# Split factors for the first tile's h from chunk 6 on, splits made by GpSimd and accumulating transfers, in a linear attention with a rational feed-forward on one Trainium2 core

## The chip, the cores and the metric

The program runs on one core of a Trainium2 chip (trn2). The metric is the time of the whole program on the device in microseconds, as the median of several runs; profiles come from one execution each. The engines are PE (TensorE), ACT (ScalarE), DVE (VectorE), POOL (GpSimd) and SP (SyncE, which issues most transfers).

## The reference

```python
# q, k, v: 8 x 8 x 576 x 64 (batch, heads, seq, head_dim); w_in: 512 x 2048; w_out: 2048 x 512
kv = einsum('bhsd,bhse->bhde', k, v)
out = einsum('bhsd,bhde->bhse', q, kv)
out = out / sqrt(mean(out * out, axis=-1) + 1e-6) * g_norm
x = out.transpose(0, 2, 1, 3).reshape(4608, 512)
h = x @ w_in
P = a[0] + a[1] * h + a[2] * h**2 + a[3] * h**3
Q = 1.0 + abs(b[0]) * abs(h) + abs(b[1]) * h**2
return (P / (Q + 1e-6)) @ w_out
```

The inputs of the attention are float32; the weights reach the kernel as float64 words, two 32-bit words per number.

## The kernel before

The 4608 rows are worked in nine tiles of 512 (t), and d_ff in 16 chunks of 128 (c). A *slot* is one pair (t, c), in a fixed order; the loop near the end of the kernel writes one slot after the other, and every engine executes its instructions in the order in which they are written. In slot i the elementwise work of h(t, c) runs on ACT and DVE (`ew_a` to `ew_d`), PE adds the product of g of two slots before into four accumulators (`gemm2`, LAG = 2), takes a step of the attention of tile t + 1 (kvp, op, ms), and makes h of the next slot (`gemm1`). h lies in a PSUM tag of two buffers, so the h after next waits until DVE has read h for the last time (L495).

PE multiplies float32 in two ways. From *unsplit* factors a block of 128 x 128 x 512 is one float32 matmul (L471, L534; the trace shows two records of it). From *split* factors, where a number is the sum of a high and a low part in float32r, it is three matmuls (L475 to L477: high weight by low x, low by high, high by high). Before, all of tile 0 is unsplit, and all later tiles are split.

Weights come in 16 units of two chunks, `("wi", c)` of w_in and `("wo", c)` of w_out. A table, `schedule`, gives each unit the slots in which it is fetched by SP (1 MB of float64), converted to float32 and split; -1 stands for the start. Conversion before: ACT scales the high words (L192), GpSimd writes the signs (`signs`, L225), ACT scales the low words, DVE shifts (L229) and adds in two halves (L233). The manual dependence `beside` holds GpSimd's signs until DVE has made q (L487). A split before is ACT's copy to float32r (L246, the high part), GpSimd's negative of it (L253), and a transfer that adds the float32 value to this (L254, `accum_op=ALU.add`), which leaves the low part.

SBUF cells are named by tags: `g0` to `g7` take raw units and later high parts, `f0` to `f15` float32 units and later low parts, `xA` and `xB` the split x of a tile in two groups of two head pairs (`split`, L293), and x of tile 0, `x0`, lies in `xB`:

```python
xs[t, p // 2] = xpool.tile([P, 2, 2, TW], F32R, tag=("xA", "xB")[p // 2], name=f"x_{t}_{p}")
```

A tile's x can be written into its cell when the last h of the tile before has read that cell.

Of the kernel before, what the change touches and what calls it, by code (L numbers as in the profile page):

```python
# [24 lines left out]
def linear_attention_then_rational_ffn(  # L25
# [97 lines left out]


    schedule = {
        ("wi", 0): (None, None, 11),
        ("wi", 2): (None, None, 12),
        ("wo", 0): (None, None, 13),
        ("wi", 4): (-1, 0, 14),
        ("wo", 2): (-1, 1, 15),  # L130
        ("wi", 6): (-1, 2, 16),
        ("wo", 4): (-1, 3, 17),
        ("wi", 8): (0, 4, 18),
        ("wo", 6): (0, 5, 19),
        ("wi", 10): (1, 6, 20),
        ("wo", 8): (2, 7, 21),
        ("wi", 12): (3, 8, 22),
        ("wo", 10): (4, 9, 23),
        ("wi", 14): (5, 10, 24),
        ("wo", 12): (6, 11, 25),  # L140
        ("wo", 14): (7, 12, 26),
    }
# [7 lines left out]
    order = []
    for c in range(NF):
        order += [(("wo", c - c % 2), c % 2)]
        order += [(("wi", c + 3 - (c + 3) % 2), (c + 3) % 2)] if c + 3 < NF else []
    made = {k: order[2 * k:2 * k + 2] for k in range(NF - 3)}
    for k, part in zip(range(NF - 3, NF), order[2 * (NF - 3):]):
        made[k] = [part]

    def unsplit(t, c):  # L160
        return t == 0
# [1 line left out]

    raws, ups, w32, whl, gparts = {}, {}, {}, {}, {}

    def fetch_w(u):
        kind, c = u
        k = units.index(u) % NG  # L170
        raws[u] = wpool.tile([P, 2 * DM], I64, tag=f"g{k}", name=f"raw_{kind}{c}")
        src = w_in[c:c + 2].rearrange("c p k f -> p c (k f)") if kind == "wi" else \
            w_out[c:c + 2].rearrange("c p f -> p c f")
        to = raws[u].rearrange("p (c f) -> p c f", c=2)
        for js in ((slice(0, 1), slice(1, 2)) if u in units[:2] else (slice(0, 2),)):
            nc.sync.dma_start(to[:, js], src[:, js])
# [11 lines left out]
    def scale(engine, to, of, by):  # L188
        if engine == "V":
            DVE.tensor_scalar(to, of, by, None, ALU.mult)  # L190
        else:
            ACT.activation(to, of, AF.Copy, scale=by)  # L192

    def conv_a(u, part=both, engine="S"):
        low, high = words(u, part)
        scale(engine, f32(high), f32(high), 2.0**-112)
        to = low if u in units[:2] else ups[u].bitcast(U16).rearrange("p (f w) -> p f w", w=2)[:, part, 0]
        scale(engine, to, low.bitcast(U32), 2.0**-29)

    def room(u):  # L200
        kind, c = u
        if u not in ups:
            ups[u] = wpool.tile([P, 2 * DM], F32, tag=f"f{units.index(u)}", name=f"{kind}w{c}")
            for j in range(2):
# [10 lines left out]
    def conv_add(u, part):
        w = ups[u].bitcast(I32)[:, part]
        DVE.tensor_tensor(w, w, words(u, part)[0], ALU.add)

    def conv_b2(u, part):
        conv_or(u, part)  # L220
        conv_add(u, part)


    def signs(u):
        return POOL.tensor_scalar(room(u), f32(words(u, both)[1]), 0.0, None, ALU.mult)  # L225

    def conv_shift(u):
        high = words(u, both)[1]
        DVE.tensor_scalar(high, high, 3, None, ALU.logical_shift_left)  # L229

    def conv_c(u, part):
        w = ups[u].bitcast(I32)[:, part]
        DVE.tensor_tensor(w, w, words(u, part)[1], ALU.add)  # L233

    def gpart(k, j):
        if k not in gparts:
            gparts[k] = wpool.tile([P, 2, 2 * DM], F32R, tag=f"g{k}", name=f"parts{k}")
        return gparts[k][:, j]

    def split_w(u):  # L240
        kind, c = u
        i = units.index(u)
        w = ups.pop(u)
        fpart = lambda k, what: wpool.tile([P, 2 * DM], F32R, tag=f"f{k}", name=f"{kind}{what}{c}")
        wh = gpart((i + 2) // 2, i % 2) if i < NU - 2 else fpart(i + 2, "h")
        ACT.copy(wh, w)  # L246

        def rest():
            wl = gpart(0, i) if i < 2 else fpart(i - 2, "l")
            for j in range(2):  # L250
                js = slice(j * DM, (j + 1) * DM)
                whl[kind, c + j] = wh[:, js], wl[:, js]
            POOL.tensor_scalar(wl, f32(wh), -1.0, None, ALU.mult)  # L253
            POOL.dma_start(wl, w, accum_op=ALU.add)  # L254
        return rest

# [33 lines left out]

    def split(t, p):  # L293
# [4 lines left out]
        ACT.copy(xh, f)
        x.setdefault(t, []).append((xh, xl))

        def rest():
            DVE.tensor_tensor(xl, f, f32(xh), ALU.subtract)
        return rest
# [163 lines left out]
    def gemm1_part(t, c, ph, cs):  # L467
        for kc in range(NPAIR):
            ks = slice(kc * P, (kc + 1) * P)
            if t == 0:  # L470
                PE.matmul(ph, w32["wi", c][:, ks], x0[:, kc, cs], start=(kc == 0), stop=(kc == NPAIR - 1))  # L471
# [3 lines left out]
            PE.matmul(ph, wh, xl, start=(kc == 0), stop=False)  # L475
            PE.matmul(ph, wl, xh, start=False, stop=False)  # L476
            PE.matmul(ph, wh, xh, start=False, stop=(kc == NPAIR - 1))  # L477


    def ew_a(t, c, ph, w=TW):  # L480
        nm = f"{t}_{c}"
# [3 lines left out]
        ACT.activation(d, ph, AF.Square)  # L485
# [1 line left out]
        q_made = DVE.scalar_tensor_tensor(q, d, b1abs, q, ALU.mult, ALU.add)  # L487
# [171 lines left out]
    conv_b1(u1, one)  # L659
    conv_b2(u1, one)  # L660
    conv_b1(u1, two)
    conv_shift(u2)


    slots = [(t, c) for t in range(NTILE) for c in range(NF)]
    beside = mybir.DependencyInfo(mybir.DependencyClass.Sync, mybir.DependencyReason.DATA)
    ph = gemm1(0, 0)
    for i, (t, c) in enumerate(slots[:-1]):
        q_made = ew_a(t, c, ph)
        for u in at_slot(1, i + 1):  # L670

            tc.add_manual_dep(signs(u).ins, q_made.ins.name, beside, reason="signs beside h")
        if i:
            ew_d(*slots[i - 1])
# [84 lines left out]
```

## Time and profile before

| | |
|---|---|
| median of 3 runs | 895.58 us (895.52 to 895.6) |
| profiled execution | 895.59 us, of which the span from first to last instruction is 893.8 |
| PE, PEld busy | 886.1 us (99%), 680.1 us (76%) |
| DVE, ACT, POOL busy | 774.0 us (87%), 696.6 us (78%), 114.4 us (13%) |
| granted TensorE clock | 1.00 throughout |

PE is the row of matmuls, PEld that of weight loads, which overlap them. Busy times are means over stages with different limits: the change touches the first tile (some 20 to 140 us) and the slots around it, and what it is worth is read there. A row of the chain or of a timeline begins with its start and its duration in microseconds; `[1.10 <-DVE q L487]` is the idle time before it and what ended this. A row of waits gives the sum, the number of times and the longest. All line numbers are those of the kernel before.

### The profile page before, as it was taken

How to read it: one execution, taken by the hardware profiler on the slowest of the kernel's cores; microseconds unless marked ns; L12 is line 12 of the kernel's file. 1: busy time of each engine (PE TensorE's matmuls, PEld its weight loads, DVE VectorE, ACT ScalarE, POOL GpSimd, SP SyncE). 2: the span in 40 equal slices, each digit the busy share in tenths (PEclk: the TensorE clock that was granted, in tenths of full speed). 3: DMA queues.
4: the chain of work that ended last, by engine and by line, in shares of the span. 5: the costliest groups of instructions: out<-in, count | busy, mean ns of one | idle time of the engine just before them, and what ended most of it. 6: DMA issues, size and time to landing. Idle time of an engine off the chain costs nothing.

```text
span 893.8 us, 11734 instructions
## 1 busy us (share of the span) xinstructions
PE 886.1 (99%) x4294; PEld 680.1 (76%) x4294; DVE 774.0 (87%) x1223; ACT 696.6 (78%) x1171; POOL 114.4 (13%) x95
## 2 busy tenths in 40 slices
PE   8999999999999999999999999999999999999998
PEld 6444446878887888878887888788878887888886
DVE  3988898989978898889978997899779988898887
ACT  5898878988886788777877787768767887777665
POOL 2644465663000000000000000000000000000000
PEclk9999999999999999999999999999999999999999
DMA  9864047754230203220320132011201020201001
GB/s 366 351 259 177 25 95 187 177 101 102 70 123 19 49 20 110 83 49 1 130 79 23 30 118 84 12 49 71 72 13 49 0 71 12 49 1 47 1 1 48
DMA packets 26266, 74.30 MB, mean 83 GB/s; under 512 B 2592, under 2 KB 2592, under 8 KB 26208
## 3 DMA queue, kind: packets, MB, share of 16 engines
q1 hardware_dynamic: 23328, 64.10, 20.9%
q0 software_dynamic: 2304, 8.39, 5.0%
q10 hardware_dynamic: 576, 1.05, 0.3%
q8 instruction: 34, 0.56, 0.2%
q14 instruction: 24, 0.20, 0.1%
HBM read 55.58 MB, written 9.57 MB: 73 GB/s over the span
## 4 chain that ended last, share of the span: by engine, by line
PE 97%; DMA 1%; DVE 1%; ACT 0%; issue 0%; SPq 0%; DVEq 0%; ACTq 0%
PE h L475 14%; PE h L477 13%; PE h L476 13%; PE acc L538 13%; PE acc L539 13%; PE acc L540 13%; PE acc L534 6%; PE h L471 5%; PE kvp L332 2%; DMA first<-in_first_dram 1%; PE ms L400 1%; PE op L383 1%; PE op L384 1%; PE op L382 1%; PE op L378 0%; DVE x L658 0%
## 5 line engine op out<-in xcount | busy, mean ns | idle before, releaser
L475 PE MATMUL h<-x,parts 128*128 128x512 f32 (+1 forms) x516 | 203.5, 394 | 0.0
L477 PE MATMUL h<-x,parts 128*128 128x512 f32 (+1 forms) x516 | 200.3, 388 | 0.0
L485 ACT ACTIVATE d<-h 128x512 f32<-128x512 f32 x143 | 85.6, 599 | 146.1 <-PE h L477 144.3
L539 PE MATMUL acc<-wol,gh 128*128 128x512 f32 x508 | 197.7, 389 | 0.0
L487 DVE SCALAR_TENSOR_TENSOR q<-d,b1abs,q 128x512 f32<-128x512 f32 x143 | 107.2, 749 | 91.1 <-ACT q L486 90.2
L476 PE MATMUL h<-x,wil 128*128 128x512 f32 (+1 forms) x388 | 150.4, 388 | 0.0
L538 PE MATMUL acc<-parts,gl 128*128 128x512 f32 x384 | 149.4, 389 | 0.0
L540 PE MATMUL acc<-parts,gh 128*128 128x512 f32 x384 | 149.4, 389 | 0.0
L475 PEld LDWEIGHTS h<-x,parts 128*128 128x128 f32 x516 | 96.9, 188 | 25.5 <-DVE gl L522 5.9
L498 ACT ACTIVATE d<-q,bias 128x512 f32<-128x512 f32 x143 | 105.6, 739 | 12.8 <-DVE q L487 10.8
L488 ACT ACTIVATE u<-h,na 128x512 f32<-128x512 f32 x143 | 112.6, 787 | 0.0
L477 PEld LDWEIGHTS h<-x,parts 128*128 128x128 f32 x516 | 96.9, 188 | 20.5
L539 PEld LDWEIGHTS acc<-wol,gh 128*128 128x128 f32 x508 | 95.4, 188 | 19.8
L499 ACT ACTIVATE d<-d,bias 128x512 f32<-128x512 f32 x143 | 103.6, 724 | 4.7
L505 DVE SCALAR_TENSOR_TENSOR u<-u,na,d 128x512 f32<-128x512 f32 x143 | 106.7, 746 | 0.0
L495 DVE SCALAR_TENSOR_TENSOR u<-u,na,h 128x512 f32<-128x512 f32 x143 | 106.1, 742 | 0.6
L503 DVE SCALAR_TENSOR_TENSOR q<-q,d 128x512 f32<-128x512 f32 x143 | 98.5, 689 | 0.2 <-ACT d L499 0.2
L489 DVE TENSOR_TENSOR u<-u,h 128x512 f32<-128x512 f32 x143 | 98.0, 686 | 0.4
L486 ACT ACTIVATE q<-h,abg 128x512 f32<-128x512 f32 x143 | 98.0, 685 | 0.0
L511 DVE SCALAR_TENSOR_TENSOR u<-q,u 128x512 f32<-128x512 f32 x127 | 91.7, 722 | 2.4
L522 DVE TENSOR_TENSOR gl<-u,gh 128x512 fp32r<-128x512 f32 x127 | 86.9, 684 | 0.0
L521 ACT CAST gh<-u 128x512 fp32r<-128x512 f32 x127 | 80.3, 632 | 4.1 <-DVE u L511 4.1
(146 smaller groups left out, 1226.6 us busy)
## 6 DMA issues: line engine op xcount, KB each, us to landing
kvm<-in_kv_dram SPq DMA_DIRECT2D x28, 640.0 KB
raw_wo<-in_w_out_dram SPq DMA_DIRECT2D x8, 1024.0 KB
qr<-in_qT_dram SPq DMA_DIRECT2D x32, 256.0 KB
out_dram<-ob SPq DMA_DIRECT2D x16, 512.0 KB
rb<-rd SPq DMA_DIRECT2D x28, 256.0 KB
raw_wi<-in_w_in_dram SPq DMA_DIRECT2D x6, 1024.0 KB
wol<-wow POOLq DMA_DIRECT2D x8, 512.0 KB, 5.3
wil<-wiw POOLq DMA_DIRECT2D x6, 512.0 KB, 4.6
```

Source lines behind the costliest of these rows:

```text
L475: PE.matmul(ph, wh, xl, start=(kc == 0), stop=False)
L476: PE.matmul(ph, wl, xh, start=False, stop=False)
L477: PE.matmul(ph, wh, xh, start=False, stop=(kc == NPAIR - 1))
L487: q_made = DVE.scalar_tensor_tensor(q, d, b1abs, q, ALU.mult, ALU.add)
L488: ACT.activation(u, ph, AF.Identity, bias=na[:, 2:3], scale=na[:, 3:4])
L495: DVE.scalar_tensor_tensor(u, u, na[:, 1:2], ph, ALU.add, ALU.mult)
L498: ACT.activation(d, q, AF.Ln, bias=bias[:, 2:3], scale=QSC)
L499: ACT.activation(d, d, AF.Exp, bias=bias[:, 3:4], scale=-1.0)
L505: DVE.scalar_tensor_tensor(u, u, na[:, 0:1], d, ALU.add, ALU.mult)
L538: PE.matmul(o, gl[:, ss], wh, start=(c == 0), stop=False)
L539: PE.matmul(o, gh[:, ss], wl, start=False, stop=False)
L540: PE.matmul(o, gh[:, ss], wh, start=False, stop=(c == NF - 1))
```

## The change

- Tile 0's h is made from split w_in and split x from chunk 6 on (`EARLY = 6`): three float32r matmuls per block instead of one float32 matmul. Products with w_out stay unsplit in tile 0.
- Its x is split at the start into two groups, one in `xA`, one in a new cell `e`.
- A split is made by GpSimd and a transfer alone (`low_by_transfer`): two GpSimd passes and an accumulating transfer. ACT's copy goes. w_in 6 to 14 are split in slots 3 to 8, the other units from slot 9 on.
- GpSimd's signs go, and with them the manual dependence. ACT scales the high words by a rectifier (Prelu) with a slope that makes the negative side carry the sign; both scalings are in place. DVE shifts straight into the float32 unit and adds, for w_in 4 to 14 in one instruction over both chunks.
- Fetches, conversions and cells have a new order, and tile 1's x uses the two cells the other way round.

```diff
     schedule = {
...
+        ("wi", 4): (-1, 0, 12, "g3", "f3", ("f1", "f2")),
+        ("wi", 6): (-1, 1, 3, "g4", "f4", "g4"),
+        ("wo", 2): (-1, 1, 13, "g5", "f5", "g0"),
+        ("wi", 8): (-1, 2, 4, "g6", "f6", "g6"),
...
     def conv_a(u, part=both, engine="S"):
         low, high = words(u, part)
-        scale(engine, f32(high), f32(high), 2.0**-112)
-        to = low if u in units[:2] else ups[u].bitcast(U16).rearrange("p (f w) -> p f w", w=2)[:, part, 0]
-        scale(engine, to, low.bitcast(U32), 2.0**-29)
+        if u == units[0]:
+            scale(engine, f32(high), f32(high), 2.0**-112)
+        else:
+            ACT.activation(f32(high), f32(high), AF.Prelu, scale=2.0**-112, alpha=-(2.0**32))
+        scale(engine, low, low.bitcast(U32), 2.0**-29)
...
-        ACT.copy(wh, w)
...
+    def low_by_transfer(high, low, of):
+        POOL.tensor_scalar(high, of, 1.0, None, ALU.mult)
+        POOL.tensor_scalar(low, f32(high), -1.0, None, ALU.mult)
+        POOL.dma_start(low, of, accum_op=ALU.add)
...
-            xs[t, p // 2] = xpool.tile([P, 2, 2, TW], F32R, tag=("xA", "xB")[p // 2], name=f"x_{t}_{p}")
+            xs[t, p // 2] = xpool.tile([P, 2, 2, TW], F32R, tag=("xA", "xB")[p // 2 ^ (t == 1)], name=f"x_{t}_{p}")
...
-            if t == 0:
+            if t == 0 and c < EARLY:
                 PE.matmul(ph, w32["wi", c][:, ks], x0[:, kc, cs], start=(kc == 0), stop=(kc == NPAIR - 1))
...
+    for g, tag in enumerate(("xA", "e")):
...
+        low_by_transfer(xs[0, g][:, :, 0], xs[0, g][:, :, 1], x0[:, 2 * g:2 * g + 2])
...
-        for u in at_slot(1, i + 1):
-
-            tc.add_manual_dep(signs(u).ins, q_made.ins.name, beside, reason="signs beside h")
...
-        rest[2] += [lambda u=u: conv_shift(u) for u in shifts]
+        rest[2] += [lambda u=u: conv_b1(u, both) for u in shifts]
```

In the table the three numbers are the slots of fetch, conversion and split; then come the cells of the raw unit, the float32 unit and the parts. How the rows move, at three places:

On ACT in slot 1 (behind the copies of kv, ahead of h of chunk 2; raw_wo and raw_wi are raw units, wow the float32 unit), before:

```order
L192 ACTIVATE raw_wo_251<-raw_wo_251 128x1024
L192 ACTIVATE wow_338<-raw_wo_251 128x1024
L485 ACTIVATE d_2_408<-h_2_376 128x512
L486 ACTIVATE q_2_409<-h_2_376,abg 128x512
L488 ACTIVATE u_2_410<-h_2_376,na 128x512
```

and after:

```order
L195 ACTIVATE raw_wi_251<-raw_wi_251 128x1024
L188 ACTIVATE raw_wi_251<-raw_wi_251 128x1024
L195 ACTIVATE raw_wo_253<-raw_wo_253 128x1024
L188 ACTIVATE raw_wo_253<-raw_wo_253 128x1024
L466 ACTIVATE d_2_412<-h_2_375 128x512
L467 ACTIVATE q_2_413<-h_2_375,abg 128x512
L469 ACTIVATE u_2_414<-h_2_375,na 128x512
```

Slot 1 converts two units instead of one ahead of h of chunk 2, and slot 3 likewise.

On POOL, from the end of the start-up on (wow and wiw are float32 units, x_157 is x0, wihl the parts of a unit), before:

```order
L225 TENSOR_SCALAR wow_297<-raw_wo_155 128x1024
L225 TENSOR_SCALAR wiw_303<-raw_wi_245 128x1024
L225 TENSOR_SCALAR wow_338<-raw_wo_251 128x1024
L225 TENSOR_SCALAR wiw_370<-raw_wi_253 128x1024
L273 TENSOR_TENSOR kvl_135<-kvf,kvh_129 64x64 x2
```

and after:

```order
L234 TENSOR_SCALAR x_0_320<-x_157 128x2x512
L235 TENSOR_SCALAR x_0_320<-x_0_320 128x2x512
L236 DMA x_0_320<-x_157 128x2x512
L234 TENSOR_SCALAR x_1_324<-x_157 128x2x512
L235 TENSOR_SCALAR x_1_324<-x_1_324 128x2x512
L236 DMA x_1_324<-x_157 128x2x512
L254 TENSOR_TENSOR kvl_135<-kvf,kvh_129 64x64 x2
L234 TENSOR_SCALAR wihl_477<-wiw_408 128x1024
L235 TENSOR_SCALAR wihl_477<-wihl_477 128x1024
L236 DMA wihl_477<-wiw_408 128x1024
```

Where four signs stood, x is split in two groups, and w_in 6 behind it; the signs are gone.

On ACT at the change from tile 1 to tile 2 (xf is x in float32, x_2_0 and x_2_2 the two groups of tile 2's split x, h_1_15 the last h of tile 1), before:

```order
L499 ACTIVATE d_1_14_1813<-d_1_14_1813,bias_95 128x512 [waits Activation_49]
L298 CAST x_2_0_1853<-xf_2_0_1119 128x512 [waits PE_49]
L298 CAST x_2_0_1853<-xf_2_1_1235 128x512
L298 CAST x_2_2_1856<-xf_2_2_1380 128x512 [waits PE_49]
L298 CAST x_2_2_1856<-xf_2_3_1492 128x512
L485 ACTIVATE d_1_15_1866<-h_1_15_1840 128x512
```

and after:

```order
L479 ACTIVATE d_1_14_1877<-d_1_14_1877,bias_95 128x512 [waits Activation_49]
L279 CAST x_2_0_1917<-xf_2_0_1214 128x512 [waits PE_49]
L279 CAST x_2_0_1917<-xf_2_1_1325 128x512
L279 CAST x_2_2_1920<-xf_2_2_1466 128x512
L279 CAST x_2_2_1920<-xf_2_3_1573 128x512
L466 ACTIVATE d_1_15_1930<-h_1_15_1904 128x512
```

The second group waits for nothing of its own any more: the cell of the first group is now the one that the last h of tile 1 reads last.

More of the change, by code (lines that the diff above doesn't have):

```diff
@@ L12 @@
 U32 = mybir.dt.uint32
-U16 = mybir.dt.uint16
 AF = mybir.ActivationFunctionType
@@ L125, in linear_attention_then_rational_ffn @@
     schedule = {
[L126 to L141, printed above, removed]
[16 rows of a table added]
     }
     units = list(schedule)
-    NU = len(units)
-    NG = NU // 2
     def at_slot(step, k):
         return [u for u in units if schedule[u][step] == k]
[L152 to L158, printed above, removed]
+    made = {0: [("wo", 0, 0), ("wi", 2, 1)]}
+    for c in range(1, NF):
+        made[c] = [("wo", c - c % 2, c % 2)]
+    for c in range(4, NF, 2):
+        made[schedule["wi", c][1] + 1].append(("wi", c, None))
+    EARLY = 6
     def unsplit(t, c):
         return t == 0
-    raws, ups, w32, whl, gparts = {}, {}, {}, {}, {}
+    raws, ups, w32, whl = {}, {}, {}, {}
     def fetch_w(u):
         kind, c = u
-        k = units.index(u) % NG
-        raws[u] = wpool.tile([P, 2 * DM], I64, tag=f"g{k}", name=f"raw_{kind}{c}")
+        raws[u] = wpool.tile([P, 2 * DM], I64, tag=schedule[u][3], name=f"raw_{kind}{c}")
         src = w_in[c:c + 2].rearrange("c p k f -> p c (k f)") if kind == "wi" else \
@@ L202, in room @@
         if u not in ups:
-            ups[u] = wpool.tile([P, 2 * DM], F32, tag=f"f{units.index(u)}", name=f"{kind}w{c}")
+            ups[u] = wpool.tile([P, 2 * DM], F32, tag=schedule[u][4], name=f"{kind}w{c}")
             for j in range(2):
@@ L217, in conv_add @@
         DVE.tensor_tensor(w, w, words(u, part)[0], ALU.add)
[L219 to L238, printed above, removed]
     def split_w(u):
         kind, c = u
-        i = units.index(u)
         w = ups.pop(u)
[L244 to L255, printed above, removed]
+        cells = schedule[u][5]
+        if isinstance(cells, str):
+            hl = wpool.tile([P, 2, 2 * DM], F32R, tag=cells, name=f"{kind}hl{c}")
+            wh, wl = hl[:, 0], hl[:, 1]
+        else:
+            wh, wl = (wpool.tile([P, 2 * DM], F32R, tag=g, name=f"{kind}{n}{c}") for g, n in zip(cells, "hl"))
+        for j in range(2):
+            js = slice(j * DM, (j + 1) * DM)
+            whl[kind, c + j] = wh[:, js], wl[:, js]
+        low_by_transfer(wh, wl, w)
+    def low_by_transfer(high, low, of):
+        POOL.tensor_scalar(high, of, 1.0, None, ALU.mult)
+        POOL.tensor_scalar(low, f32(high), -1.0, None, ALU.mult)
+        POOL.dma_start(low, of, accum_op=ALU.add)
     kvslot = {}
@@ L486, in ew_a @@
         ACT.activation(q, ph, AF.Abs, scale=b0)
-        q_made = DVE.scalar_tensor_tensor(q, d, b1abs, q, ALU.mult, ALU.add)
+        DVE.scalar_tensor_tensor(q, d, b1abs, q, ALU.mult, ALU.add)
         ACT.activation(u, ph, AF.Identity, bias=na[:, 2:3], scale=na[:, 3:4])
@@ L490, in ew_a @@
         pend[t, c] = (d, q, u)
-        return q_made
     def ew_b(t, c, ph, fill):
@@ L636, in linear_attention_then_rational_ffn @@
     conv_b1(u0, one)
-    conv_b2(u0, one)
+    conv_or(u0, one)
+    conv_add(u0, one)
     conv_a(u0, two, "V")
@@ L646, in linear_attention_then_rational_ffn @@
     conv_add(u0, two)
-    signs(u2)
     conv_a(u1, one)
     conv_a(u1, two)
-    for u in at_slot(1, 0):
-        signs(u)
     conv_a(u2)
@@ L658, in linear_attention_then_rational_ffn @@
         DVE.scalar_tensor_tensor(x0[:, p], x0[:, p], ghalf, rb, ALU.mult, ALU.mult)
[L659 to L662, printed above, removed]
+    conv_b1(u1, both)
+    conv_add(u1, one)
+    conv_b1(u2, both)
+    for g, tag in enumerate(("xA", "e")):
+        xs[0, g] = xpool.tile([P, 2, 2, TW], F32R, tag=tag, name=f"x_0_{g}") if g == 0 else \
+            wpool.tile([P, 2, 2, TW], F32R, tag=tag, name=f"x_0_{g}")
+        low_by_transfer(xs[0, g][:, :, 0], xs[0, g][:, :, 1], x0[:, 2 * g:2 * g + 2])
+        x.setdefault(0, []).extend((xs[0, g][:, p, 0], xs[0, g][:, p, 1]) for p in range(2))
     slots = [(t, c) for t in range(NTILE) for c in range(NF)]
-    beside = mybir.DependencyInfo(mybir.DependencyClass.Sync, mybir.DependencyReason.DATA)
     ph = gemm1(0, 0)
     for i, (t, c) in enumerate(slots[:-1]):
-        q_made = ew_a(t, c, ph)
-        for u in at_slot(1, i + 1):
-            tc.add_manual_dep(signs(u).ins, q_made.ins.name, beside, reason="signs beside h")
+        ew_a(t, c, ph)
         if i:
@@ L676, in linear_attention_then_rational_ffn @@
         shifts = []
-        convs = [lambda u=u, j=j: (conv_b2 if u == u1 else conv_c)(u, (one, two)[j]) for u, j in made.get(i, [])]
+        convs = [lambda u=(k, n), j=j: conv_add(u, both if j is None else (one, two)[j]) for k, n, j in made.get(i, [])]
         ew_b(t, c, ph, convs[:1])
@@ L683, in linear_attention_then_rational_ffn @@
                 evacuate(slots[i - LAG][0])
-        for u in at_slot(2, i) if i >= NF else []:
-            rest[2].append(split_w(u))
+        for u in at_slot(2, i):
+            split_w(u)
         if i < 4:
@@ L698, in linear_attention_then_rational_ffn @@
         rest[2] += convs[1:]
-        for u in at_slot(2, i) if i < NF else []:
-            rest[2].append(split_w(u))
         if t == 0 and c == NF - 3:
```

12 rows, old and new, of the table schedule are left out of this document.

## The prediction

> **What bounds the kernel now.** I read the page first, then the chain that ended last, then the waits and the timelines of the places that the change touches.
>
> ```profile
> span 893.8 us, 11734 instructions
> PE 886.1 (99%) x4294; PEld 680.1 (76%) x4294; DVE 774.0 (87%) x1223; ACT 696.6 (78%) x1171; POOL 114.4 (13%) x95
> PE 97%; DMA 1%; DVE 1%; ACT 0%; issue 0%; SPq 0%; DVEq 0%; ACTq 0%
> ```
>
> PE is busy for 99% of the span and 97% of the chain: work taken from PE shortens the time by its full length wherever the others keep up, and a wait of PE lengthens it by its full length. In the chain, ordered by time, these pieces carry the sum:
>
> ```profile
> 29.29 0.76 DVE u L495
> 30.09 3.70 PE h L471 x8
> 61.64 0.73 PE kvp L332 x20
> 62.37 3.63 PE h L471 x8
> 128.44 3.43 PE h L471 x8
> 135.31 0.23 PE h L475
> ...
> 137.84 0.23 PE h L477
> 138.07 3.43 PE acc L534 x8
> ```
>
> An h chunk from unsplit factors (L471) takes 3.43 us; one from split factors (twelve pieces, L475 to L477) takes 138.07 - 135.31 = 2.76. PE has one wait behind the start-up, for DVE in front of h of chunk 2:
>
> ```profile
> PEld h L471 <- DVE u L495: 1.3, 1, 1.3
> ```
>
> **A. Split h, chunks 6 to 15.** Ten chunks go from 3.43 to 2.76 us: 10 x 0.67 = -6.7 us, all on PE.
>
> **B. Start.** Chunk 2 takes the PSUM buffer that DVE L495 releases.
>
> ```profile
> 24.33 1.17 DVE L209 TENSOR_SCALAR wiw<-raw_wi 128x512 int32<-128x512 int32 x1
> ...
> 26.36 0.69 DVE L217 CUSTOM_DVE_ANT_0 wiw<-raw_wi,wiw 128x1024 uint16<-128x1024 uint16 x1
> ...
> 27.31 0.70 DVE L229 TENSOR_SCALAR raw_wo<-raw_wo 128x1024 int32<-128x1024 int32 x1
> 24.16 1.15 ACT L192 ACTIVATE raw_wo<-raw_wo 128x1024 f32<-128x1024 f32 x1 [2.47 <-POOL wow L225]
> 26.41 0.58 ACT L485 ACTIVATE d<-h 128x512 f32<-128x512 f32 x1
> ```
>
> Five DVE instructions, from 24.33 to about 27.9 (27.31 and the step of 0.6 between rows), become three: a shift of 1024 (0.70), an addition (0.69), a shift (0.70). ACT no longer waits 2.47 us for GpSimd's signs. DVE's q could then start near 26.7, when ACT has made its inputs from h of chunk 0, instead of 27.9: 1.2 us earlier, which is nearly all of PE's 1.3. Bounds 0 and -1.3; since GpSimd now runs beside it (D), I take -1.1.
>
> **C. Chunk 6: is its split there in time?** Its second pass (low part of w_in) comes at 62.37 + 0.23, less 1.1: 61.5. Ahead of it: slot 1 now has two conversions on ACT, then DVE's addition at the end of slot 2, two GpSimd passes, and the transfer.
>
> ```profile
> 35.26 0.72 ACT L498 ACTIVATE d<-q,bias 128x512 f32<-128x512 f32 x1 [1.10 <-DVE q L487]
> 37.31 1.17 ACT L192 ACTIVATE raw_wo<-raw_wo 128x1024 f32<-128x1024 f32 x1
> ...
> 39.76 0.60 ACT L485 ACTIVATE d<-h 128x512 f32<-128x512 f32 x1
> 45.01 0.69 DVE L511 SCALAR_TENSOR_TENSOR g<-q,u 128x512 f32<-128x512 f32 x1
> 45.62 0.68 DVE L233 CUSTOM_DVE_ANT_0 wiw<-raw_wi,wiw 128x1024 uint16<-128x1024 uint16 x1
> 138.57 3.32 POOL L253 TENSOR_SCALAR wol<-parts 128x1024 fp32r<-128x1024 f32 x1 [2.84 <-ACT parts L246]
> 143.93 2.98 POOL L253 TENSOR_SCALAR wil<-parts 128x1024 fp32r<-128x1024 f32 x1 [0.84 <-ACT parts L246]
> 147.20 0.90 POOL L254 DMA_DIRECT2D wil<-wiw  x1 [0.30 <-POOL wil L253]
> wol<-wow POOLq DMA_DIRECT2D x1, 512.0 KB, 8.8
> wil<-wiw POOLq DMA_DIRECT2D x1, 512.0 KB, 4.5
> 55.24 0.38 SPq L176 DMA_DIRECT2D raw_wo<-in_w_out_dram  x1
> ```
>
> The two rows of transfers are DMA answers for 140 to 152 us, with loads and stores beside it, and for 185 to 187, alone. A conversion costs ACT 39.76 - 37.31 = 2.45 us. Slot 2 there starts at 39.76, less 1.2 (earlier start), plus 2.45, less 0.7 (most of the 1.10 wait is swallowed): about 40.3. So g of slot 2 ends near 45.70 + 0.55, or 0.7 later if one GpSimd pass stops DVE (D); I take 46.5. The addition, now of 2048 halfwords instead of 1024, takes twice the step of 0.6 between the two DVE rows: 47.7. GpSimd takes 2 x (3.15, the middle of its two rows, + 0.30 before the next): issue at 54.6. Landing 4.5 later is 59.1, no wait; 8.8 later is 63.4, a wait of 1.9. I take the late one, because a 1 MB weight load starts at the same moment (55.24) and the 8.8 had such company: +1.9. Bounds 0 and +5: the addition half a slot later, or the transfer wholly behind those loads. A first share of this wait can show one step earlier, at kvp of pair 2 (61.64 less 1.1), whose PSUM bank ACT has to empty: ACT comes there 2 x 2.45 - 1.2 - 0.7 = 3 us later than before.
>
> **D. What GpSimd's passes do to DVE.**
>
> ```profile
> 139.30 1.41 DVE L511 SCALAR_TENSOR_TENSOR g<-q,u 128x512 f32<-128x512 f32 x1
> 146.19 0.68 DVE L511 SCALAR_TENSOR_TENSOR u<-q,u 128x512 f32<-128x512 f32 x1
> 145.77 3.43 PE acc L534 x8
> 120.00:130.00 10.00, 10.00 (x25) 4.38 (x24) 9.82 (x16) 6.01 (x10) 6.72 (x4) 1.00 0.51 116
> ```
>
> The first row lies 0.7 us behind the start of C's pass at 138.57, the second meets none: a DVE instruction with two SBUF inputs that meets the beginning of a pass takes 1.41 instead of 0.68, 0.7 us more. The signs of before start beside instructions that read PSUM and meet none. Now slots 0 to 8 hold 14 passes (four for x, ten for w_in), up to 14 x 0.7 = 10 us of DVE; up to chunk 6 they are in C's 0.7, behind it attention leaves PE's slots longer than DVE's. In the last slots DVE is full (9.82 of 10; the row is PE, PEld, DVE, ACT, POOL, clock): per slot of 6.87 us 6.75, now 7.45 against 6.2 for PE. Over three slots it falls back 3.7 us; g of chunk 15, which ends at 139.30 + 1.41, is used by the chain's L534 at 145.77, 5.1 later. So 0 here, +3 at worst. [...]
>
> **E. New map of cells.** For tile 1 the two x tiles change cells, so tile 2's first x needs the cell that h of (1,15) reads last instead of first.
>
> ```profile
> 227.60 1.15 ACT L298 CAST x<-xf 128x512 fp32r<-128x512 f32 x2
> 228.96 1.15 ACT L298 CAST x<-xf 128x512 fp32r<-128x512 f32 x2 [0.21 <-PE h L477]
> 228.54 0.68 DVE L302 TENSOR_TENSOR x<-xf,x 128x512 fp32r<-128x512 f32 x1
> 233.47 0.68 DVE L522 TENSOR_TENSOR gl<-u,gh 128x512 fp32r<-128x512 f32 x1
> 234.21 0.50 PE L538 MATMUL acc<-woh,gl 128*128 128x512 f32 x1
> ```
>
> The first cast moves from 227.60 to 228.96 and ends at 229.6; DVE's subtraction goes from 228.54 to 229.6, and L522, behind it without a gap, from 234.15 to 235.2. PE takes its result at 234.21, so nothing is in hand: +1.05. Bounds 0 (a gap on DVE that I do not see) and +1.4.
>
> **Moved fetches, and the rest.** SP's queue keeps its length: w_in 6 goes ahead of w_out 2, w_out 4 behind w_in 10, and the last w_out between the stores of rd and the loads of rb; two x transfers of 512 KB join the loads at about 30 and 37 us. I cost this at 0, covered by the one to three slots of 7 us between a fetch and its conversion; with that cover gone, ACT would wait at its conversion, ahead of C's chain, and the wait would be C's. Two passes per unit instead of ACT's copy and one pass: ACT is freed of one copy per unit, in slots that PE bounds: 0. From slot 16 on a unit comes every second slot with two passes instead of every slot with one: the same number of stops. The sign by a rectifier instead of a copy: the same 1024 elements, 0 (bounds under the rivals).
>
> **Sum.** -6.7 - 1.1 + 1.9 + 0 + 1.05 = -4.85 us, against the profiled execution's 895.59, 0.01 above the median of the runs: 890.7.
>
> **Rivals.** Faster or slower means by over 0.2% (1.8 us), about what a measurement of this kernel can tell from none.
> - *All hidden* (C is 0): 888.8. For it: 4.5 us alone; against it: the loads beside it. 0.15.
> - *The gain is eaten at chunk 6* (C from 4.9 to 8): 893.8 to 896.9. For it: four steps in a row, each of which can only be late; against it: no transfer row above 8.8. 0.17.
> - *DVE late at the end of the tile* (D +3): 893.5. For it: 9.82 of 10; against it: 5.1 in hand. 0.05, mostly faster.
> - *Slower: the rectifier costs ACT more.* Two functions above differ by 0.14 us on 512 columns (26.41, 35.26), 0.3 for 1024; the far end is a change of tables.
>
> ```profile
> 2.88 1.28 ACT L67 ACT_TABLE_LOAD   x1 [2.88 <-issue]
> 32.35 0.56 ACT L485 ACTIVATE d<-h 128x512 f32<-128x512 f32 x1
> 59.95 0.58 ACT L485 ACTIVATE d<-h 128x512 f32<-128x512 f32 x1
> ```
>
> From h of chunk 1 to h of chunk 5 ACT took 27.6 us (32.35 to 59.95) with four conversions; with six it needs 27.6 + 2 x 2.45 = 32.5, and PE's four slots take 32.3 (30.09 to 62.37). Each 0.1 us per rectifier delays ACT by 0.6 with little in hand. At 0.3 that is 1.8 us and goes into C's wait; from about 1.1 on (6.6 us, and each later slot overfull too) it is slower, and with two table loads per use (2.56, 15 us in these slots) 900 to 910. Against it: the changed program lists one table load in all, as before. 0.11.
> - *Not what it says:* a missed dependence that keeps h as long as before; the program's rows show three passes per block. 0.03, no change.
> [...]
>
> **How the numbers follow.** The forecast has 0.47. Faster: 0.47 + 0.15 + 0.03 = 0.65; same: 0.17 + 0.02 + 0.03 = 0.22; slower: 0.11 + 0.02 = 0.13. The range goes from the hidden case with B at its bound and E smaller, 888.0, to most of the eaten case, 896.0.
>
> **What would show it.** h of chunk 6 to 15 at 2.75 us; no wait of PE for L495 at 29 us; a wait of 1 to 3 us near 61, for the transfer of low w_in, part of it perhaps for ACT before kvp; one of 1 us near 227 for DVE; rectifier rows of 1.15 to 1.2 us; DVE instructions of 1.4 us beside GpSimd in the first tile. Wrong it would be if the rectifier's rows are above 1.6, if transfers in 50 to 65 us take over 12 us, or if PE waits for g near 130.

## The result and the profile after

The changed kernel takes 905.95 us (median of 4 runs, 905.55 to 906.35) against 895.55 for the kernel before (895.5 to 895.6): a ratio of 1.0116 (95% interval 1.0099 to 1.0134), 10.4 us slower. Forecast were 890.7. These lines of the page after answer to the first three of the prediction: span, busy time by engine, and the chain's shares.

```profile
span 903.9 us, 11786 instructions
PE 882.2 (98%) x4334; PEld 686.3 (76%) x4334; DVE 792.7 (88%) x1214; ACT 677.3 (75%) x1155; POOL 133.5 (15%) x103
PE 81%; DVE 13%; ACT 3%; issue 2%; DMA 1%; SPq 0%; DVEq 0%; ACTq 0%
```

PE's busy time is less by 3.9 us, where A had 6.7 (the run without weight passes below has 879.7, so 6.4 less; the matmuls of tile 0 take 2.5 us more here than there). DVE, with nine instructions fewer than before, is busy 18.7 us longer, and now carries 13% of the chain (1% before). The windows say where. Columns: stretch, length, then busy time (and instructions) of PE, PEld, DVE, ACT, POOL, then clock and DMA. First before, then after:

```profile
100.00:120.00 20.00, 20.00 (x48) 8.88 (x47) 18.54 (x28) 18.62 (x24) 11.79 (x5) 1.00 0.24 60
120.00:140.00 20.00, 20.00 (x53) 9.85 (x52) 18.98 (x29) 14.46 (x23) 11.80 (x7) 1.00 0.47 99
140.00:160.00 20.00, 20.00 (x115) 14.71 (x114) 16.31 (x27) 18.08 (x33) 12.27 (x7) 1.00 0.81 211
```

```profile
100.00:120.00 20.00, 17.18 (x57) 10.35 (x56) 19.71 (x22) 13.43 (x20) 18.75 (x9) 1.00 0.66 156
120.00:140.00 20.00, 16.50 (x49) 8.84 (x48) 19.67 (x26) 11.40 (x18) 17.49 (x9) 1.00 0.38 82
140.00:160.00 20.00, 16.52 (x92) 10.10 (x92) 19.59 (x27) 11.77 (x23) 18.04 (x9) 1.00 0.64 153
```

PE was never idle there; now it stands 9.8 of 60 us. DVE is full, and it does so with fewer instructions: 75 against 84. Its instructions have become longer. The seven largest waits of PE behind the start-up (total, times, longest, us):

```profile
PE h L456 <- DVE u L475: 4.2, 2, 2.3
PE acc L514 <- DVE g L491: 3.2, 3, 1.2
PE h L456 <- DVE x L283: 1.5, 1, 1.5
PE h L457 <- DMA wihl<-wiw: 1.4, 1, 1.4
PE kvp L313 <- ACT xf L369: 1.3, 1, 1.3
PE op L363 <- DVE ql L348: 0.9, 1, 0.9
PE acc L518 <- DVE gl L502: 0.9, 1, 0.9
```

Five of the seven name DVE. The timelines of ACT, DVE and POOL near 130 to 143 us show how DVE got long (start, duration, engine, line, operation):

```profile
129.48 1.16 ACT L195 ACTIVATE raw_wo<-raw_wo 128x1024 f32<-128x1024 f32 x1
131.42 2.19 DVE L491 SCALAR_TENSOR_TENSOR g<-q,u 128x512 f32<-128x512 f32 x1
131.70 3.11 POOL L234 TENSOR_SCALAR woh<-wow 128x1024 fp32r<-128x1024 f32 x1
136.67 1.52 DVE L468 SCALAR_TENSOR_TENSOR q<-d,b1abs,q 128x512 f32<-128x512 f32 x1
136.26 3.11 POOL L235 TENSOR_SCALAR wol<-woh 128x1024 fp32r<-128x1024 f32 x1 [1.46 <-DMA wohl<-wow]
140.09 2.12 DVE L483 SCALAR_TENSOR_TENSOR q<-q,d 128x512 f32<-128x512 f32 x1
140.29 3.11 POOL L234 TENSOR_SCALAR wohl<-wow 128x1024 fp32r<-128x1024 f32 x1
```

Each of these GpSimd passes has a lengthened DVE instruction at its beginning: 2.19, 1.52 and 2.12 us for forms that else take 0.69 to 0.75. Summed over 20 to 240 us (duration above the usual one of the same line and shape, for DVE instructions that overlap a pass), the 36 passes after cost DVE 30 us in 35 instructions: 21 lose 0.6 to 1.0 (16.7 us), nine lose 1.1 to 1.7 (12.6 us), five lose less than 0.3. Before, 30 passes cost 8.6 us in 12 instructions, none above 1.0. The rectifier (L195) takes 1.16 us, no more than the copy (1.17 for the same shape before; medians of 14).

How far PE is behind the kernel before, at the same matmuls (start of a chunk of `acc` in tile 0 minus its start before, us; the last column is the difference of the spans). The lower rows are experiments told below:

| kernel | chunk 0 | 3 | 4 | 9 | 13 | 15 | span |
|---|---|---|---|---|---|---|---|
| after | -0.38 | +0.88 | +3.26 | -0.17 | +1.96 | +7.76 | +10.1 |
| no weight passes | -0.38 | +0.83 | +0.18 | -3.25 | -6.05 | -6.08 | -5.0 |
| fills for passes | -0.25 | +0.95 | +4.63 | +1.53 | -1.27 | -1.30 | -0.2 |
| passes beside q, last version | -0.48 | -0.49 | +0.05 | -2.50 | -5.30 | -5.34 | -5.1 |

After gains from chunk 4 to 9, at the full rate of the split h, and then gives it all back and more.

### The profile page after: what moved, and what is told of

The parts are those of the page before. It is cut to its first block, busy times and chain, and to the rows that moved or that the text cites. A ratio compares the mean times of both kernels' runs of the same rounds, so it can differ in the third digit from the quotient of the medians.

```text
span 903.9 us, 11786 instructions
## 1 busy us (share of the span) xinstructions
PE 882.2 (98%) x4334; PEld 686.3 (76%) x4334; DVE 792.7 (88%) x1214; ACT 677.3 (75%) x1155; POOL 133.5 (15%) x103
## 3 DMA queue, kind: packets, MB, share of 16 engines
q10 hardware_dynamic: 576, 1.05, 0.3%
## 4 chain that ended last, share of the span: by engine, by line
PE 81%; DVE 13%; ACT 3%; issue 2%; DMA 1%; SPq 0%; DVEq 0%; ACTq 0%
PE h L456 13%; PE h L458 12%; PE h L457 12%; PE acc L518 12%; PE acc L519 12%; PE acc L520 12%; DVE q L468 2%; PE kvp L313 2%; DVE q L483 2%; DVE wow L215 1%; DVE u L485 1%; DVE u L475 1%; DMA first<-in_first_dram 1%; DVE u L470 1%; PE op L364 1%
## 5 line engine op out<-in xcount | busy, mean ns | idle before, releaser
L468 DVE SCALAR_TENSOR_TENSOR q<-d,b1abs,q 128x512 f32<-128x512 f32 x143 | 114.5, 801 | 83.5 <-ACT q L467 82.7
L456 PE MATMUL h<-x,wihl 128*128 128x512 f32 (+1 forms) x364 | 144.6, 397 | 1.8 <-DVE u L475 1.8
L457 PE MATMUL h<-x,wihl 128*128 128x512 f32 (+1 forms) x364 | 141.1, 388 | 1.4 <-DMA wihl<-wiw 1.4
L458 PE MATMUL h<-x,wihl 128*128 128x512 f32 (+1 forms) x364 | 141.0, 387 | 0.0
L475 DVE SCALAR_TENSOR_TENSOR u<-u,na,h 128x512 f32<-128x512 f32 x143 | 105.9, 741 | 0.6
L483 DVE SCALAR_TENSOR_TENSOR q<-q,d 128x512 f32<-128x512 f32 x143 | 104.1, 728 | 0.2 <-ACT d L479 0.2
L518 PE MATMUL acc<-woh,gl 128*128 128x512 f32 x256 | 99.6, 389 | 0.0
L519 PE MATMUL acc<-wol,gh 128*128 128x512 f32 x256 | 99.6, 389 | 0.0
L520 PE MATMUL acc<-woh,gh 128*128 128x512 f32 x256 | 99.6, 389 | 0.0
L518 PE MATMUL acc<-wohl,gl 128*128 128x512 f32 x252 | 98.1, 389 | 0.9 <-DVE gl L502 0.9
L519 PE MATMUL acc<-wohl,gh 128*128 128x512 f32 x252 | 98.0, 389 | 0.0
L520 PE MATMUL acc<-wohl,gh 128*128 128x512 f32 x252 | 98.0, 389 | 0.0
L491 DVE SCALAR_TENSOR_TENSOR u<-q,u 128x512 f32<-128x512 f32 x127 | 89.7, 706 | 2.4
L456 PEld LDWEIGHTS h<-x,wihl 128*128 128x128 f32 x364 | 68.4, 188 | 24.4 <-DVE gl L502 5.9
```

The lines of the kernel that those rows point to most:

```text
L475: DVE.scalar_tensor_tensor(u, u, na[:, 1:2], ph, ALU.add, ALU.mult)
L483: DVE.scalar_tensor_tensor(q, q, QEPS, d, ALU.add, ALU.mult)
L518: PE.matmul(o, gl[:, ss], wh, start=(c == 0), stop=False)
L519: PE.matmul(o, gh[:, ss], wl, start=False, stop=False)
L520: PE.matmul(o, gh[:, ss], wh, start=False, stop=(c == NF - 1))
```

## The experiments

Theory: GpSimd's passes stop DVE, DVE has no room for that in the last slots of tile 0, and PE waits for it. Rivals: the late transfers at chunk 6 (C), the map of cells (E), the split h itself, ACT. Times of the kernel before beside these runs were 895.49 to 895.56 us.

**1. Both weight passes on ACT.**
```diff
-        low_by_transfer(wh, wl, w)
+        ACT.copy(wh, w)
+        ACT.activation(wl, f32(wh), AF.Copy, scale=-1.0)
+        POOL.dma_start(wl, w, accum_op=ALU.add)
```


> Both passes of every weight block (copy of the high part, negative of it) go from GpSimd to ACT; GpSimd keeps the four passes of x and the transfers. Theory (GpSimd's passes stop DVE, and DVE has become what the first tile waits for): the time that DVE loses beside GpSimd between 20 and 240 us falls from 30 to under 9 us, DVE's share in 60 to 160 us falls from 98% to about 92%, the waits of PE for g and u there go, and the time falls by the 12 to 15 us that PE stood: 891 to 894. ACT gets 32 x 1.15 = 37 us more in the first 180 us, of which it had 42 free, so 3 us may be lost to it: up to 897. Rival 1 (the late transfers, not the stops): the same transfers start at the same points, 904 to 907. Rival 2 (the map of cells, or the split h itself): 904 to 907.

907.9 us (ratio 1.0127, 1.011 to 1.0144): no gain, all expectations missed. DVE did lose little beside passes (2.8 us), but ACT took the loss over. The runs lie between 906.8 and 911.2 us, and the rows are of the longest of them. The first is PE's longest wait, the second what ACT stood for:

```profile
PE op L365 <- DVE ql L350: 6.4, 1, 6.4
ACT wol L232 <- DMA wohl<-wow: 5.8, 1, 5.8
```

ACT's copy goes into a cell that an earlier block's transfer still reads; GpSimd could stand there at no cost, ACT has the next chunk's functions behind it. The run decides nothing on the stops.

**2. High part on ACT, the one GpSimd pass begun beside q.** The copy is issued one slot ahead, by `split_w`, which gives back GpSimd's pass and the transfer; the pass waits for DVE's q, behind which two instructions read PSUM.
```diff
+        for f in lows.pop(i, []):
+            neg, move = f()
+            tc.add_manual_dep(neg.ins, q_made.ins.name, beside, reason="low beside h")
+            move()
...
-        for u in at_slot(2, i):
-            split_w(u)
+        for u in at_slot(2, i + 1):
+            lows.setdefault(i + 1, []).append(split_w(u))
```


> ACT copies the high part of each weight block one slot earlier, and GpSimd's one remaining pass per block waits for DVE's q, so that it begins beside two DVE instructions that read PSUM (the addition of a w_in block is put ahead of that of a w_out block). Theory of the stops: 16 weight passes instead of 32, and nearly all begin where they stop nothing: DVE loses under 8 us instead of 30, PE's waits for g and u go, 889 to 893. If only the number of passes counts, not where they begin: half of the loss, about 15 us, and 897 to 900. Rival (late transfers, map of cells): 904 to 907, or later still since w_in's transfers do not start earlier by more than 2 us.

903.1 us (1.0085, 1.007 to 1.01): 2.8 faster than after, much less than either figure expected. 20 passes cost DVE 4.5 us instead of 30 for 36, so beginning a pass there does avoid most stops. But PE now waits for ACT, which in slots 2 to 5 has a copy besides one or two conversions and stands for DVE's addition before it (five times, 5.3 us):

```profile
PE op L363 <- ACT kvf L252: 4.5, 3, 3.2
```

**3. h unsplit up to chunk 9** (`EARLY = 10` for 6).

> Chunks 6 to 9 of the first tile's h take the unsplit factors again (3.43 us on PE instead of 2.76, four chunks: +2.7 us of PE's work); all splits are made as before. Theory (DVE is the bound in the first tile): PE's extra work lies in its waits, and the wait for the transfer near 61 us (1.4 us) goes too: 904.5 to 906.5, no change. If PE is still the bound there: 908.6. If the late transfer at chunk 6 is what costs: under 902.

906.5 us (1.0122, 1.0107 to 1.0137), where after had 905.95: 2.7 us more work for PE cost about 0.5. At chunk 9 the kernel is 1.4 us later than after, at the end 0.8. What PE gains in these chunks has no worth while DVE sets the end of the tile.

**4. The map alone.**
```diff
-            xs[t, p // 2] = xpool.tile([P, 2, 2, TW], F32R, tag=("xA", "xB")[p // 2 ^ (t == 1)], name=f"x_{t}_{p}")
+            xs[t, p // 2] = xpool.tile([P, 2, 2, TW], F32R, tag=("xA", "xB")[p // 2 ^ (t >= 1)], name=f"x_{t}_{p}")
```


> The two x tiles keep from tile 1 on the cells that tile 1 gave them, so tile 2's first x has its cell back where the kernel before had it. All theories: PE's wait of 0.9 us for gl near the end of tile 1 goes, 905.0 (904.5 to 905.5). If the map were the main cost: under 900.

904.8 us (1.0103, 1.0088 to 1.0118), 1.2 less than after: PE's wait for gl (0.9) is gone from the list. As expected.

**5. No weight passes at all.**
```diff
-        low_by_transfer(wh, wl, w)
+        POOL.dma_start(wh, w)
+        POOL.dma_start(wl, w)
```


> The two GpSimd passes of every weight block become two plain transfers of the block (so the low part holds the block itself, not the remainder); nothing is added to ACT or DVE, and h of chunks 6 to 15 still takes split factors. x keeps its four passes. Theory (the stops of DVE behind GpSimd's passes eat the gain): DVE loses under 5 us beside passes instead of 30, PE's waits for g and u in 100 to 160 us go, 890 to 895. Rival (DVE's own work in the last slots of the first tile is more than PE's shortened slots, stops or not): the waits near 132 to 146 us stay in part, and the time comes out between, 896 to 901. Rival (the stops cost nothing that ends on PE): 904 to 907.

890.57 us (0.9946, 0.9929 to 0.9962). The gain that the change was forecast to have is there as soon as the 32 passes are not. The page's span and busy line, and one window:

```profile
span 888.8 us, 11772 instructions
PE 879.7 (99%) x4334; PEld 686.9 (77%) x4334; DVE 765.6 (86%) x1214; ACT 676.4 (76%) x1155; POOL 41.4 (5%) x87
```
```profile
120.00:140.00 20.00, 20.00 (x102) 12.44 (x101) 19.01 (x32) 12.49 (x24) 4.20 (x8) 1.00 0.63 210
```

The same 1214 DVE instructions as after take 27.1 us less, and PE is full again. DVE is still at 19.0 of 20: this stretch has room for its own work and for nothing else. Since the transfers also start earlier here, the next but two separates them.

**6. All passes beside q, h unsplit to chunk 9, later splits.** As 2, with `EARLY = 10`, the map of 4, w_in 6 to 12 split one slot later, and x's four passes beside q of chunks 0 to 3.

> High parts by ACT one slot ahead and every GpSimd pass begun beside DVE's q, x's four passes too; h of chunks 0 to 9 unsplit; w_in's splits one slot later from chunk 6 on; the map of the third kernel of the call before. Against the run that had passes beside q (903.1) it takes ACT's copies out of the slots 2 to 5, where ACT had two conversions each, so the waits of PE for ACT there (5.5 us) should go, and 1.1 us of the map: 896 to 897 by that alone. Theory of the stops alone: 890 to 893. If DVE's own work at the end of the tile is the limit: 894 to 898.

894.9 us (0.9991, 0.9982 to 1.0001), no difference from before. It was 4.2 us ahead at chunk 13 and lost 3.3 by chunk 14. Some 20 us earlier ACT had stood for a cell once more; whether that is the cause is what the next version tests (9):

```profile
112.06 1.05 ACT L231 CAST wih<-wiw 128x1024 fp32r<-128x1024 f32 x1 [3.80 <-DMA wil<-wiw]
```

**7. Additions of w_out left out.**
```diff
     def conv_add(u, part):
+        if u[0] == "wo" and u[1] >= 2:
+            return
```


> The additions of the low words of all w_out blocks but the first are left out (14 DVE instructions of 0.6 us per step in slots 2 to 15; the weights lose their low words); passes and everything else as in the changed kernel. Theory (DVE is the bound of the first tile): 5 to 8 of the 8.4 us come off, 898 to 901. If PE's lateness comes from transfers, ACT or the map: 905 to 906.

901.5 us (1.0067, 1.0052 to 1.0082): 4.5 of the 8.4 us of DVE's work come off, just outside the expected range. At chunk 4 this kernel is 4.9 us behind, where after is 3.3, with a wait of 2.5 us for w_in's transfer; from chunk 9 to 15 it loses 1.2 us, where after loses 7.9. It speaks for DVE as the bound there: work that only DVE has was taken away.

**8. Fills in the place of passes.**
```diff
-        low_by_transfer(wh, wl, w)
+        last = slice(2 * DM - 8, 2 * DM)
+        POOL.tensor_copy(wh[:, last], w[:, last])
+        for part in (wh, wl):
+            for _ in range(3):
+                POOL.memset(f32(part)[:, 0:2 * DM - 8], 0.0)
+        POOL.tensor_copy(wl[:, last], wh[:, last])
+        POOL.dma_start(wl, w, accum_op=ALU.add)
```


> GpSimd stays as busy beside DVE as in the changed kernel, and each low part's accumulating transfer starts about when it did, but the two passes of a weight block are replaced by six fills with zero of 0.95 us (and two copies of 8 columns, which hold the place behind DVE's addition). The high parts are zero, so the output is not the product. Theory (the stops, and fills stop nothing): DVE loses under 8 us, and the time is that of the run without passes (890.6) plus what the later transfers cost at chunk 6, 0 to 3 us: 890.5 to 893.5. Rival (the gain of the run without passes came from its earlier transfers, or from a free GpSimd queue): 900 to 906.

895.57 us (1.0003, 0.9994 to 1.0012): 10.4 us less than after, 5.0 more than without passes, so above the range of the theory and below that of its rival. One window, and the longest wait of PE:

```profile
120.00:140.00 20.00, 20.00 (x64) 11.70 (x63) 19.71 (x30) 14.48 (x23) 17.11 (x21) 1.00 0.39 82
```
```profile
PE h L463 <- DMA wihl<-wiw: 2.6, 1, 2.6
```

GpSimd is as busy as after (17.11 against 17.49), DVE does 30 instructions where it did 26, PE is full. So it is not a busy GpSimd but what its instructions do that costs. Most of the 5.0 is C: by the table PE goes from +0.95 to +4.63 between chunks 3 and 4, and stays 4.4 to 4.8 behind the kernel without passes up to the end of the tile.

**9 and 10. Later splits, and h unsplit to chunk 7.** From 6, with `EARLY = 8`; the splits of w_in 4 and of w_out from 2 on one slot later (9), those of w_out 8 to 14 two slots later (10).

> As the run with all passes beside q, but h is unsplit up to chunk 7 instead of 9, and the splits from the fourth w_in block on come one slot later, so that ACT's copy no longer stands 3.8 us in front of a cell that a transfer still reads. Theory: of that run's lateness at the end of the first tile (3.3 us between chunks 13 and 14) nearly all goes, and two more chunks gain 0.67 each: 894.9 - 3.3 - 1.3 = 890.3 (889.5 to 892). If DVE's own work in the last slots is the limit: 893 to 895.

898.85 us (1.0039, 1.0026 to 1.0051). It is 5.3 us ahead at chunk 15, so the loss at chunk 14 is gone with that wait; then the wait had moved to a later block:

```profile
146.63 1.04 ACT L231 CAST woh<-wow 128x1024 fp32r<-128x1024 f32 x1 [7.08 <-DMA wol<-wow]
```

> As the kernel before it, with the splits of w_out blocks 8 to 14 one slot later still, so that ACT's copy for block 8 no longer stands 7.1 us in front of a cell that block 4's transfer reads. At chunk 15 that kernel was 5.3 us ahead of the one before the change, and lost 9 to the wait. Theory (stops gone, ACT never held): the 5.3 us stay, 890.2 (889.5 to 891.5), faster than both. If the wait only moves to the next block: 893 to 899.

890.5 us (890.37 to 890.67; 0.9943, 0.993 to 0.9957): 5.1 us faster than the kernel before, 15.4 faster than the change.

```profile
span 888.7 us, 11761 instructions
PE 879.8 (99%) x4326; PEld 685.1 (77%) x4326; DVE 767.2 (86%) x1214; ACT 692.2 (78%) x1171; POOL 83.5 (9%) x87
```

Again the same 1214 DVE instructions, 25.5 us shorter in all than after; POOL's 20 passes cost DVE 2.9 us.

**11. The price of a pass by itself.** DVE in an unbroken row, GpSimd beside it.

> Only DVE instructions in an unbroken row with GpSimd passes beside them, in six stretches: DVE reads two SBUF inputs, with GpSimd copies of 128x1024, 128x512 and 128x256 and fills of 128x1024; then DVE shifts of 128x1024, and DVE with one input from PSUM, both with copies of 128x1024. The output is all zeros. If a pass stops DVE for its first part only: about one lengthened DVE instruction of 1.4 to 2.2 us per pass, whatever its width, so that narrow passes cost more per element; none with an input from PSUM. If DVE is stopped for a share of the whole pass: the loss falls with the width. If only reading does it: none beside fills.

Timeline rows, in the order: DVE with no pass beside it; DVE and a copy of 1024 columns; of 512; fills; a shift beside a copy; one input from PSUM beside a copy.

```profile
19.73 0.69 DVE L53 SCALAR_TENSOR_TENSOR a<-b,a 128x512 f32<-128x512 f32 x1
7.43 1.41 DVE L53 SCALAR_TENSOR_TENSOR a<-b,a 128x512 f32<-128x512 f32 x1
6.80 3.22 POOL L57 TENSOR_SCALAR hi<-src 128x1024 f32<-128x1024 f32 x1
31.83 0.98 DVE L53 SCALAR_TENSOR_TENSOR a<-b,a 128x512 f32<-128x512 f32 x1
31.21 1.94 POOL L57 TENSOR_SCALAR hi<-src 128x512 f32<-128x512 f32 x1
78.89 3.60 DVE L53 SCALAR_TENSOR_TENSOR a<-b,a 128x512 f32<-128x512 f32 x5
78.96 3.98 POOL L61 MEMSET hi<- 128x1024 f32 x4
104.07 1.40 DVE L64 TENSOR_SCALAR a<-b 128x1024 int32<-128x1024 int32 x1
105.50 1.40 DVE L64 TENSOR_SCALAR a<-b 128x1024 int32<-128x1024 int32 x1
132.09 0.69 DVE L53 SCALAR_TENSOR_TENSOR a<-b,ps 128x512 f32<-128x512 f32 x1
```

A copy of 1024 columns makes one DVE instruction lose 0.72 us; 512 columns 0.29; 256 columns (not shown) 0.21. The loss falls with the width, so it is not a fixed entry fee. Fills: five instructions in 3.60 us, none lost. A shift of 1024 columns, with one SBUF input, is stopped twice per pass (1.43 us). An input from PSUM: nothing lost. So beside an instruction with two SBUF inputs the copies, which read SBUF, cost 0.72 us of a pass of 2.8 to 3.2, and the fills, which read nothing, cost none.

**12 to 14. Where the pass begins.** First a pass released by DVE's instruction, as in the kernel, with none to three instructions behind it reading PSUM; then passes put off in steps of 32 columns of a fill; then DVE's instructions made independent of one another.

> DVE in an unbroken row; a GpSimd copy of 128x1024 is released by the end of a DVE instruction, as behind an addition in the kernel, four times each with the next DVE instructions reading: SBUF only; PSUM in the first; PSUM in the first two; PSUM in the first three. The output is all zeros. Theory (the price is set by what DVE reads at the start of the pass): SBUF only 1.4 us lost per pass as in the kernel's rows of 2.1 us, one from PSUM 0.7 or less, two or three none. If the pass stops whatever reads two SBUF inputs at any time within its 2.8 us: 0.7 to 1.4 lost in all four.

```profile
13.71 1.41 DVE L53 SCALAR_TENSOR_TENSOR a<-b,a 128x512 f32<-128x512 f32 x1
45.39 0.91 DVE L53 SCALAR_TENSOR_TENSOR a<-b,a 128x512 f32<-128x512 f32 x1
68.03 0.69 DVE L53 SCALAR_TENSOR_TENSOR a<-b,ps 128x512 f32<-128x512 f32 x1
67.36 2.77 POOL L60 TENSOR_SCALAR hi<-src 128x1024 f32<-128x1024 f32 x1 [4.78 <-DVE src L59]
```

The rows: SBUF only, one from PSUM ahead, two ahead. 0.72, 0.22 and 0 us lost, for every pass of each kind but the first of the second (0.15): behind two instructions that read PSUM, 1.4 us in all, a pass cost nothing. The 1.4 us expected for SBUF only did not come.

> DVE in an unbroken row on two SBUF inputs; sixteen GpSimd copies of 128x1024, each put off by a fill of 0, 32, ... 480 columns, so that they begin at different points of a DVE instruction. The output is all zeros. Theory: the point decides between the two prices seen in the kernel: a pass that begins 0.1 to 0.4 us after a DVE instruction stretches that one by 1.4 us, one that begins at its start or end the next by 0.7. Rival (the 1.4 us come from something else in the kernel, not the point): every pass costs 0.7 us.

All sixteen passes cost 0.72 to 0.77 us, begun 0.23 to 0.61 us after a DVE instruction; it is always the next one that is stretched. In this row the point does not decide; the rival held. In the kernel after the two prices do go with the point: the 21 stops of 0.6 to 1.0 us fall on an instruction that starts behind the pass, eight of the nine dearer ones on an instruction into which the pass begins, 0.03 to 0.33 us after its start. What makes the kernel differ from this row stays open.

> As the kernel before it, but DVE's instructions write four tiles in turn and read none that another of them writes, so that they follow one another every 0.60 us as in the kernel, not every 0.72. The output is all zeros. If the overlap of one DVE instruction with the next decides the price: some of the sixteen passes cost 1.2 to 1.5 us, the rest 0.7. If not: 0.7 each, and the dearer stops of the kernel stay unexplained.

```profile
24.54 1.52 DVE L57 SCALAR_TENSOR_TENSOR o<-b,a 128x512 f32<-128x512 f32 x1
24.32 2.94 POOL L65 TENSOR_SCALAR hi<-src 128x1024 f32<-128x1024 f32 x1
13.37 7.30 DVE L57 SCALAR_TENSOR_TENSOR o<-b,a 128x512 f32<-128x512 f32 x12
13.71 9.59 POOL L65 TENSOR_SCALAR hi<-src 128x1024 f32<-128x1024 f32 x1
```

Eight of the sixteen passes stretched one DVE instruction from 0.68 to 1.52, just what the kernel shows at 136.67; the other eight stretched none and took 8.6 to 9.6 us themselves: the one shown ends 2.6 us, about a pass, after DVE's row (13.71 + 9.59 against 13.37 + 7.30). No pass cost 1.4. So nine of after's 35 stops, with 12.6 of its 30 us, are of a size that no run by itself has shown. What makes them dearer stays open.

## Why the prediction was wrong

**The step that failed is D, "0 here, +3 at worst".** By the table its term is +12.0: between chunks 9 and 15 after loses 7.93 where the kernel without weight passes gains 2.83, which is 10.8, and another 1.2 up to h of tile 1 (among it PE's 0.9 for ql). x's four passes cost 1.3 more (-0.38 at chunk 0 to +0.88 at chunk 3; beside q -0.48 to -0.49). The half of the step on the slots with attention held: from chunk 4 to 9 after gains 3.43, as much as the kernel without weight passes. Three things in the other half were off:
- *The price.* 0.7 was read from one row. 21 of the 35 stops are of that kind, nine take twice as much. And not all signs of before met nothing: at 24.33 DVE's shift L209 took 1.17 us, beside a sign pass begun at 24.11, where the same shape took 0.42 at 26.97.
- *The count.* The step counted 14 passes in slots 0 to 8, and for the last slots one stop each (6.75 to 7.45 us), though from slot 9 to 16 there is a block, so two passes, in every slot. With two stops its own figures give 8.15 against 6.2 us, some 2 us in each of the six slots from chunk 9 to 15 (an estimate). Before, ten passes in 100 to 160 us cost 3 us; after, sixteen cost 14. They follow an addition or each other, and so begin where an instruction with two SBUF inputs comes next.
- *The hand.* "5.1 in hand" was read at g alone. PE also waited for u (L475), which frees h's PSUM buffer, for x's remainder (L283) and for ql: 4.2, 1.5 and 0.9 us against 3.2 for g. What is in hand is the smallest of these, and DVE at "9.82 of 10" was the warning: the prediction saw it and let the shorter slot of PE pass as a lag to be made up.

The rival "DVE late at the end of the tile" was the right mechanism; it was sized at +3 and 0.05. The sign "PE waits for g near 130", given as what would make the prediction wrong, came: 1.15 us at 132.5.

**The other terms.** A: forecast -6.7; without passes -0.65 at chunk 6 and -6.23 over the next nine, -6.9. E: +1.05 forecast; PE's lag without passes grows by 1.06 there, and the map put back gives 1.2. C: +1.9 forecast; +2.38 from chunk 3 to 4 although h of chunk 6 saves 0.65, so 3.0 (0 with early transfers, 4.3 with fills), within the bounds; it shows as waits for ACT ahead of kvp (1.3) and for the transfer (1.4), as the prediction said. The transfer was issued at 56.64, not 54.6, and took 9.8 us, more than any row of before (8.8). B: -1.1 forecast; -0.38 at chunk 0, and x's passes, which the step left out, take that back. The step had DVE's q start near 26.7, but ACT now stood for h of chunk 0, and its two functions ahead of q end near 27.5:

```profile
26.30 0.60 ACT L466 ACTIVATE d<-h 128x512 f32<-128x512 f32 x1 [2.46 <-PE h L452]
27.51 0.75 DVE L468 SCALAR_TENSOR_TENSOR q<-d,b1abs,q 128x512 f32<-128x512 f32 x1 [0.92 <-ACT q L467]
```

The measured terms, -0.4 + 1.3 - 6.9 + 3.0 + 12.0 + 1.1, give 10.1, the difference of the spans; they are cut out of the same table, so the sum has to come out.

The rival that spoke of another engine fell: the rectifier is not dearer (1.16 us against 1.17). The 0.02 beside the 0.11 in the chance of "slower" would need DVE stopped for as long as a whole pass, and no run shows that: where GpSimd comes first, the runs show a quarter of the pass by itself (0.72 of 2.8 us), at most about half in the kernel (1.73 of 3.27), and nothing beside fills.

The 890.7 forecast and the 890.6 without weight passes agree partly by chance: that run has no C, and keeps x's passes. So does the 890.5 of the last version, which leaves two more chunks unsplit and has the map put back.

## What to carry to other kernels

A GpSimd pass over SBUF was not free here for being off the critical path (36 passes cost DVE 30 us): count what it takes from DVE, by where each pass begins, and compare it with DVE's idle time in that very stretch. Beginning the pass beside two DVE instructions that read PSUM made it nearly free here (2.9 us for 20 passes); moving it to ACT was worse (907.9 us against 905.95), as long as ACT could stand behind a transfer for a cell. And when one engine's slot is made shorter, look at every result that it takes from the next engine, buffers included, not at the one with the most in hand.

## What the runs showed of the hardware

- By itself a GpSimd copy made one DVE instruction with two SBUF inputs longer by 0.72 us for 128x1024 (a pass of 2.8 to 3.3 us), 0.29 for 128x512 (1.94) and 0.21 for 128x256; in nine of 35 cases of the kernel it was 1.1 to 1.7 for 128x1024; a shift with one SBUF input of 128x1024 lost 1.43 per pass. Beside fills instructions with two SBUF inputs lost nothing (five in 3.60 us), nor did one with an input from PSUM beside copies (0.69 us).
- It goes the other way too: beside DVE instructions that follow each other every 0.60 us, eight of sixteen passes took 8.6 to 9.6 us, where another took 2.94; the one shown ended 2.6 us after DVE's row.
- The rectifier with a slope for negative inputs took 1.16 us for 128x1024, the copy of the same shape before 1.17 (medians of 14).
- Accumulating transfers of 512 KB took 4.5 to 11.1 us from issue to landing, before and after. Where one still read the cell that ACT was to write next, ACT stood 3.3, 3.8, 5.8 and 7.1 us in four kernels.
